# A decode block's backward pass: V transposed on TensorE as 32-bit words, and dP summed over even and odd features

## The chip, the cores and the metric

The kernel runs on one core of a Trainium2 chip. A core has five engines that run side by side and wait for each other through semaphores: TensorE (PE: matrix products and transposes, whose result always goes to the PSUM memory), VectorE (DVE), ScalarE (ACT), GpSimd (POOL) and SyncE (SP), which here only issues DMA transfers. A TensorE product has two halves in the profile: the load of the stationary operand (LDWEIGHTS, shown as PEld) and the pass of the moving operand (MATMUL, shown as PE). Sixteen DMA engines move data between the device memory (HBM) and the on-chip memory (SBUF, 128 partitions).

The metric is the time of one execution on the device in microseconds. The kernel before takes 1698.24 us (median of 3 runs, 1697.31 to 1698.51).

## The reference, cut to what matters

The program is one transformer block for a single new token, with its forward pass and the gradients of all inputs. There are 4 batches and 32 heads, so 128 pairs (b, h), called heads below and numbered s = 0 to 127; each has its own cached keys and values of 4096 rows by 128 features in bf16 (1 MB each).

```python
q      = (layernorm(x) @ wq)                      # per head: 128 features
scores = einsum("bhqd,bhkd->bhqk", q, k_cache) * Dh ** -0.5
p      = softmax(scores)
o      = einsum("bhqk,bhkd->bhqd", p, v_cache)
h      = x + o @ wo
h2     = h + (silu(hn @ w1) * (hn @ w3)) @ w2     # hn = layernorm(h)
```

The gradients with respect to the caches are as large as the caches. For one head, with dO the gradient of its output row:

```python
dP = V @ dO                        # 4096 numbers: each row of V times dO
dS = p * (dP - sum(p * dP)) * Dh ** -0.5
grad_V = outer(p,  dO)             # 4096 x 128, 1 MB
grad_K = outer(dS, q)              # 4096 x 128, 1 MB
```

The change is in how dP is computed. The forward pass and the outer products stay.

## The kernel before, in words

**Two passes over the caches.** The forward pass (up to about 675 us of the span) reads K and V of every head once. The small dense layers follow, and from about 695 us on the backward pass reads V of every head a second time and writes grad_V and grad_K: 3 MB of transfers for each head. All these transfers are issued from SP's queue, in the order of the program. SBUF holds an arena of 23 slots (`NSLOT`), each of which has room for one head's 1 MB; a load needs a free slot, and so does an outer product before it can be written. A slot becomes free again when a store has landed or when the V in it has been used.

**How a head of V lies in SBUF.** Partition p holds 32 consecutive cache rows (j = 0 to 31) with 128 features each: 4096 bf16 numbers.

**dP of the first 32 heads** (`SP = 32`). dP sums over features, and TensorE sums over partitions, so V has to be transposed. `V_T` (lines 791 to 801) does it in four groups of `GW = 8` rows: eight TensorE transposes of 128x128 bf16 blocks (line 800) fill one PSUM tile `pt_tps`, and ScalarE copies the tile back over the V it came from (line 801). There are two such PSUM tiles, so TensorE may be one group ahead of ScalarE. `front` (line 1212) runs the four groups for a head and then eight matmuls of 512 columns (line 1228) into the accumulator `dP_ps`. They are four wide in columns: each writes 32 of the 128 PSUM partitions (`tile_position=(0, 32 * c)`), and a small stationary operand `zd`, zero except for the column that belongs to this head, puts the head's dP into its own row. `dO_window` (line 1191) writes dO into `zd` on GpSimd, two heads ahead.

After four heads the accumulator is copied to SBUF (`rows_out`, line 1203), transposed by four 128x128 fp32 transposes (`rows_T`, line 1210), and `group_dS` (line 1239) makes dS from it on VectorE. `grad_V` and `grad_K` make the outer products on VectorE (line 806) and issue the stores (lines 817 and 1255). The copies `P_pairs` (line 1198) on GpSimd lay out p for grad_V.

**dP of the other 96 heads** goes by pairs of heads, 48 of them: one 2 MB load (line 1280) puts two heads side by side, 64 partitions each. `front_pair` (line 1292) has eight groups of eight transposes (line 1298) and copies (line 1299), then 16 matmuls (line 1313). `dO_pair` (line 1287) fills their stationary operand `zt` by one GpSimd copy (line 1290), `P2_pair` (line 1376) lays out p. `grad_pair` makes an outer product of 2 MB in one VectorE instruction (line 1379) and issues one store (line 1389).

**What sets the order.** The order on each engine is written out by hand by the loops at the end of the kernel (lines 1436 to 1493): for each head or pair the loads ahead, the front of a head five ahead (three pairs ahead), the grad_V outer products some heads ahead, the grad_K outer product, and now and then a step of side work (weight gradients). Each engine runs its instructions in that order.

Of the kernel before, what the change touches and what calls it, by code (L numbers as in the profile page):

```python
# [21 lines left out]
SP = 32  # L22
# [5 lines left out]
def kernel(  # L28
# [38 lines left out]
    GW = 8  # L67
# [724 lines left out]

    def V_T(s, ps, part=range(SJ // GW)):
        if s not in VTs:
            VTs[s] = V2s.pop(s)
        v = VTs[s].heads()
        for g in part:
            pt = ps.tile([P, GW, P], BF16, tag="tps", name="pt_tps")
            for i in range(GW):
                nc.tensor.transpose(pt[:, i, :], v[:, g * GW + i, :], ident_b[:])  # L800
            nc.scalar.copy(out=v[:, g * GW:(g + 1) * GW, :], in_=pt[:])  # L801
# [163 lines left out]
    with ExitStack() as c2:  # L965
# [221 lines left out]
        zd = [bw3.tile([P, 132], BF16, name=f"zd{i}", tag=f"zd{i}", bufs=1) for i in range(B)]  # L1187
        for i in range(B):
            nc.gpsimd.memset(zd[i][:], 0.0)

        def dO_window(s):
            if s < SP:
                nc.gpsimd.tensor_copy(out=zd[s % B][:, 32:132:67], in_=dOT_bf[:, s:s + 1].to_broadcast([P, 2]))
# [18 lines left out]
        def front(s):  # L1212
# [8 lines left out]
            VT = VTs[s].heads()  # L1221
# [3 lines left out]
            for u in range(2):  # L1225
                for c in range(4):
                    j0 = 8 * c + 4 * u
                    nc.tensor.matmul(rows["acc"][32 * c:32 * (c + 1), :], lhsT=zq_window(zd[hl], 2 * hl + u),
                                     rhs=VT[:, j0:j0 + 4, :], start=(hl == 0 and u == 0),
                                     stop=(hl == B - 1 and u == 1), tile_position=(0, 32 * c))  # L1230
# [8 lines left out]
        def group_dS(g):  # L1239
            i0 = g * B  # L1240
            T = rows.pop("T").rearrange("p jj (c m) -> p c m jj", c=4)
            t = rows.pop("t")[:, 0:B * SJ].rearrange("p (b j) -> p b j", b=B)
            t5 = t.rearrange("p b (c u jj) -> p b c u jj", c=4, u=2)
            for hl in range(B):
                nc.vector.tensor_scalar(out=t5[:, hl], in0=T[:, :, 2 * hl:2 * hl + 2, :], scalar1=c_rep[:, i0 + hl:i0 + hl + 1],
# [41 lines left out]
        def dO_pair(t):  # L1287
            if t < NT:
                s, s2 = two(t)
                nc.gpsimd.tensor_copy(out=zt[t % B][:, 32:34], in_=dOT_bf[:, s:s2 + 1:B])  # L1290

        def front_pair(t, mid):
            pl = t % 2
            v = pV[t].t[:, 0:2 * SJ * Dh].rearrange("p (j d) -> p j d", d=Dh)
            for g in range(2 * SJ // GW):
                pt = psT.tile([P, GW, P], BF16, tag="tps", name="pt_tps")
                for i in range(GW):
                    nc.tensor.transpose(pt[:, i, :], v[:, g * GW + i, :], ident_b[:])  # L1298
# [225 lines left out]
```

## Time and profile before

| | before |
|---|---|
| median of 3 runs | 1698.24 us |
| the profiled execution: span, first to last instruction | 1696.2 us |
| the profiled execution's own time: span and what lies around it (no time of its own is given; the median less the span is 2.0 us) | 1698.2 us |
| instructions | 37839 |
| PE busy | 1233.4 us (73%), 16228 matmuls, 16228 weight loads |
| DVE busy | 1234.4 us (73%) |
| ACT busy | 959.5 us (57%) |
| POOL busy | 336.9 us (20%) |
| moved | 707.45 MB, mean 417 GB/s |

A busy share is the time in which an engine had an instruction in work, divided by the span. An engine can be busy for 73% and still not set the time, because its work may lie beside something longer. So one looks next for the resource that has no idle time, then for the places where even that one has gaps, and asks what ended those gaps.

### The profile page before, as it was taken

Reading aid. Unit: us, or ns where it says so; the run is one execution under the profiler, and the core shown is the slowest. Engines: PE = TensorE matmul, PEld = TensorE weight load, DVE = VectorE, ACT = ScalarE, POOL = GpSimd, SP = SyncE. Lnnn points to the kernel's source line nnn. Section 1 sums busy time; section 2 is a strip of 40 time slices with the busy share of each in tenths; the row PEclk is TensorE's granted clock in tenths of the full one; section 3 lists DMA queues with packets and bytes.
Section 4 is the critical chain, followed back from the end, with each engine's and each line's share of the span. In section 5 each row is a group of like instructions: output and inputs, shape, how many; then the busy total and the mean of one; then the engine's idle time right before and its main releaser. Section 6 shows DMA issues by size and latency. Waiting matters only on the chain.

```text
span 1696.2 us, 37839 instructions
## 1 busy us (share of the span) xinstructions
PE 1233.4 (73%) x16228; PEld 943.4 (56%) x16228; DVE 1234.4 (73%) x1198; ACT 959.5 (57%) x1490; POOL 336.9 (20%) x583
## 2 busy tenths in 40 slices
PE   5889888888888888877876755667665666766650
PEld 4777667666677666655655544444444444444440
DVE  5989999999998997667766466575665655655683
ACT  3555544454454544677665555666665666666650
POOL 1211222222222222222231121011210102011120
PEclk8999999999999999899898689886678777676675
DMA  9999999999999999999999999999999999999995
GB/s 401 424 424 424 424 424 424 424 424 423 416 423 406 424 414 397 395 414 425 425 425 429 428 429 428 429 430 429 429 429 428 418 430 429 422 418 425 415 429 230
DMA packets 81000, 707.45 MB, mean 417 GB/s; under 512 B 8748, under 2 KB 12984, under 8 KB 15296
## 3 DMA queue, kind: packets, MB, share of 16 engines
q1 hardware_dynamic: 80416, 704.94, 99.0%
q8 instruction: 127, 2.08, 0.5%
q14 instruction: 41, 0.34, 0.0%
q0 software_dynamic: 416, 0.10, 0.0%
HBM read 422.59 MB, written 282.34 MB: 416 GB/s over the span
## 4 chain that ended last, share of the span: by engine, by line
DMA 46%; DVE 9%; PE 3%; issue 2%; ACT 1%; DVEq 0%; POOL 0%; SPq 0%; ACTq 0%
DMA out_dram<-arena 43%; DVE arena L1379 7%; DMA arena<-in_A_v_cache_dram 3%; DVE arena L806 1%; PE M_ps L472 1%; DVE arena L457 1%; PE pt_w L601 0%; ACT arena L1299 0%; ACT Pn L436 0%; DVEq L1519 0%; PE kP_ps L482 0%; DVE dPr L1326 0%; PE pt_tps L1298 0%; PE gu_ps L873 0%; PE dn_ps L904 0%
## 5 line engine op out<-in xcount | busy, mean ns | idle before, releaser
L1299 ACT COPY arena<-pt_tps 128x1024 bf16<-128x1024 bf16 x384 | 369.8, 1023 | 232.3 <-PE pt_tps L1298 231.6
L1298 PE MATMUL pt_tps<-ident_b,arena 128*128 128x128 bf16 x3072 | 308.1, 272 | 204.7 <-DMA arena<-in_A_v_cache_dram 149.4
L1298 PEld LDWEIGHTS <-arena 128*128 128x128 bf16 x3072 | 263.9, 125 | 304.2 <-DMA arena<-in_A_v_cache_dram 172.8
L1379 DVE TENSOR_TENSOR arena<-arena 128x8192 bf16<-128x8192 bf16 x48 | 212.5, 4427 | 205.1 <-DMA out_dram<-arena 202.3
L472 PE MATMUL M_ps<-arena 128*128 128x130 bf16 x4096 | 285.1, 222 | 42.9 <-DMA arena<-in_A_v_cache_dram 42.2
L457 DVE TENSOR_TENSOR arena<-arena 128x4096 bf16<-128x4096 bf16 x128 | 292.5, 2285 | 23.9 <-POOL arena L453 23.9
L472 PEld LDWEIGHTS <-arena 128*128 128x128 bf16 x4096 | 251.9, 99 | 64.0 <-DMA arena<-in_A_v_cache_dram 57.2
L1379 DVE TENSOR_TENSOR arena<-dS,arena 128x8192 bf16<-128x8192 bf16 x48 | 212.3, 4424 | 73.0 <-DMA out_dram<-arena 73.0
L364 DVE STREAM_TRANSPOSE arena<-arena 128x512 f32<-128x512 f32 (+1 forms) x321 | 250.7, 797 | 0.0
L359 ACT COPY arena<-pt_tps 128x1024 bf16<-128x1024 bf16 x128 | 129.5, 1012 | 188.9 <-PE pt_tps L358 150.5
L1376 POOL COPY arena<-arena 128x128 bf16<-128x128 bf16 x48 | 55.3, 1153 | 492.3 <-ACT arena L1353 286.3
L370 POOL TENSOR_TENSOR W<-qrep,wmask 128x128 bf16<-128x128 bf16 x128 | 120.2, 939 | 85.6 <-PE S_ps L390 70.8
L801 ACT COPY arena<-pt_tps 128x1024 bf16<-128x1024 bf16 x128 | 121.7, 1025 | 26.1 <-PE pt_tps L800 24.8
L453 POOL COPY arena<-P_all 128x64 bf16<-128x64 bf16 x128 | 32.7, 255 | 412.8 <-ACT P_all L447 409.8
L806 DVE TENSOR_TENSOR arena<-dS,arena 128x4096 bf16<-128x4096 bf16 x32 | 73.2, 2293 | 35.0 <-DMA out_dram<-arena 34.7
L800 PE MATMUL pt_tps<-ident_b,arena 128*128 128x128 bf16 x1024 | 78.5, 229 | 27.1 <-ACT arena L801 27.1
L1313 PE MATMUL dP_ps<-arena 128*32 128x512 bf16 x768 | 85.7, 484 | 7.6 <-ACT arena L1299 7.3
L800 PEld LDWEIGHTS <-arena 128*128 128x128 bf16 x1024 | 67.2, 104 | 37.5 <-issue 35.9
L447 ACT COPY P_all<-pt_P 32x64 bf16<-32x64 bf16 x256 | 52.1, 204 | 53.6 <-PE pt_P L443 51.4
L806 DVE TENSOR_TENSOR arena<-P,arena 128x4096 bf16<-128x4096 bf16 x29 | 66.4, 2295 | 19.8 <-DMA out_dram<-arena 19.8
L358 PE MATMUL pt_tps<-ident_b,arena 128*128 128x128 bf16 x1024 | 80.1, 222 | 0.0
L482 PE MATMUL kP_ps<-arena,onesw 128*32 128x512 bf16 x1024 | 79.6, 388 | 0.0
(245 smaller groups left out, 1576.5 us busy)
## 6 DMA issues: line engine op xcount, KB each, us to landing
out_dram<-arena SPq DMA_DIRECT2D x96, 2048.0 KB, 27.9
arena<-in_A_v_cache_dram SPq DMA_DIRECT2D x160, 1024.0 KB, 15.9
arena<-in_A_k_cache_dram SPq DMA_DIRECT2D x128, 1024.0 KB, 15.3
arena<-in_A_v_cache_dram SPq DMA_DIRECT2D x48, 2048.0 KB, 32.1
out_dram<-arena SPq DMA_DIRECT2D x72, 1024.0 KB, 20.2
arena<-in_A_wq_dram SPq DMA_DIRECT2D x8, 1024.0 KB, 14.4
arena<-in_B_w_dram SPq DMA_DIRECT2D x8, 896.0 KB, 15.3
out_dram<-arena SPq DMA_DIRECT2D x6, 896.0 KB, 28.4
```

Of the source, the lines that this page charges most:

```text
L359: nc.scalar.copy(out=KT[:, c * GW:(c + 1) * GW, :], in_=pt[:])
L364: nc.vector.transpose(out=KT[:, c * w_:(c + n) * w_], in_=Kn[:, c * w_:(c + n) * w_])
L370: nc.gpsimd.tensor_tensor(out=W[:, hl], in0=qrep[:, :, s:s + 1].to_broadcast([P, 4, 32]), in1=wmask[:, hl, None, :].to_broadcast([P, 4, 32 ...
L457: nc.vector.tensor_tensor(out=PK[:, :, 0:Dh].rearrange("p j (r t) -> p j r t", t=2), in0=Ks[s].heads().rearrange("p j (r t) -> p j r t", t=2),
L472: nc.tensor.matmul(hold["M"][:], lhsT=Vn[:, j, :], rhs=PK[:, j, :], start=(j == 0), stop=(j == SJ - 1))
L800: nc.tensor.transpose(pt[:, i, :], v[:, g * GW + i, :], ident_b[:])
L801: nc.scalar.copy(out=v[:, g * GW:(g + 1) * GW, :], in_=pt[:])
L806: nc.vector.tensor_tensor(out=dst.rearrange("p j (r t) -> p j r t", t=2), in0=col2[:, :, None, :].to_broadcast([P, SJ, Dh // 2, 2]), in1=r ...
L1298: nc.tensor.transpose(pt[:, i, :], v[:, g * GW + i, :], ident_b[:])
L1299: nc.scalar.copy(out=v[:, g * GW:(g + 1) * GW, :], in_=pt[:])
L1313: nc.tensor.matmul(rows["acc"][32 * c:32 * (c + 1), :], lhsT=zt[t % B][:, 32 - m:64 - m], rhs=v[:, j0:j0 + 4, :], start=(pl == 0 and u == ...
L1379: nc.vector.tensor_tensor(out=dst.rearrange("p (j r t) -> p j r t", r=Dh // 2, t=2), in0=col2[:, :, None, :].to_broadcast([P, 2 * SJ, Dh / ...
```

## The change

In PSUM and in the transposes a pair of neighbouring bf16 features is handled as one 32-bit word. A head then has 16 blocks of 128x128 words in place of 32 blocks of 128x128 bf16 numbers. A block covers two cache rows with 64 feature pairs each; after its transpose, partition i * 64 + r holds feature pair r of row i of the two. `words_T` does four such transposes for a group and the same ScalarE copy of 128x1024 bf16, whose destination now is four runs of 256 numbers. The groups are interleaved: group g takes blocks g, 4 + g, 8 + g and 12 + g.

Since even and odd features now lie side by side in one partition, dP is a sum of two matmuls: one reads the even features (every second bf16 number) with the even features of dO as stationary operand, the other the odd ones. The count of matmuls stays at 8 for a head and 16 for a pair. For this dO itself is needed in word order: `dO_words` makes it by four matmuls and a ScalarE copy, once ahead of the first head and once for the pairs. A stationary operand is now filled by two GpSimd copies of 64 partitions in place of one of 128. The transposed dP has its rows in another order, and `group_dS` and `group_dS_pair` read it accordingly.

```diff
+    def words_T(ps, v, g):
+        w = v.bitcast(FP32).rearrange("p (x r) -> p x r", r=Dh)
+        pt = ps.tile([P, GW, P], BF16, tag="tps", name="pt_tps")
+        ptw = pt.rearrange("p a b -> p (a b)").bitcast(FP32).rearrange("p (x q) -> p x q", q=P)
+        for jj in range(4):
+            nc.tensor.transpose(ptw[:, jj, :], w[:, 4 * jj + g, :], ident_f[:])
+        nc.scalar.copy(out=v.rearrange("p (x n) -> p x n", n=2 * Dh)[:, g:16:4], in_=pt.rearrange("p (x i) d -> p x (i d)", i=2))
+
+    def words_of(v, g, k):
+        return v.rearrange("p (x r t) -> p t x r", r=Dh, t=2)[:, k, g:16:4]
+
     def V_T(s, ps, part=range(SJ // GW)):
...
         for g in part:
-            pt = ps.tile([P, GW, P], BF16, tag="tps", name="pt_tps")
-            for i in range(GW):
-                nc.tensor.transpose(pt[:, i, :], v[:, g * GW + i, :], ident_b[:])
-            nc.scalar.copy(out=v[:, g * GW:(g + 1) * GW, :], in_=pt[:])
+            words_T(ps, VTs[s].t[:, 0:SJ * Dh], g)
...
+        def dO_words(dst, s0, s1):
+            ps = psrep.tile([P, 2, s1 - s0], FP32, tag="rep", name="dOw_ps")
+            for k in range(2):
+                for i in range(2):
+                    nc.tensor.matmul(ps[64 * i:64 * (i + 1), k, :], lhsT=ident_b[:, k:P:2], rhs=dOT_bf[:, s0:s1],
+                                     start=True, stop=True, tile_position=(0, 64 * i))
+            nc.scalar.copy(out=dst, in_=ps[:])
+
         def dO_window(s):
             if s < SP:
-                nc.gpsimd.tensor_copy(out=zd[s % B][:, 32:132:67], in_=dOT_bf[:, s:s + 1].to_broadcast([P, 2]))
+                for i in range(2):
+                    r_ = slice(64 * i, 64 * (i + 1))
+                    nc.gpsimd.tensor_copy(out=zd[s % B][r_, :, 2 * (s % B) + i], in_=dOw[r_, :, s])
...
-            for u in range(2):
+            for k in range(2):
                 for c in range(4):
-                    j0 = 8 * c + 4 * u
-                    nc.tensor.matmul(rows["acc"][32 * c:32 * (c + 1), :], lhsT=zq_window(zd[hl], 2 * hl + u),
-                                     rhs=VT[:, j0:j0 + 4, :], start=(hl == 0 and u == 0),
-                                     stop=(hl == B - 1 and u == 1), tile_position=(0, 32 * c))
+                    nc.tensor.matmul(rows["acc"][32 * c:32 * (c + 1), :], lhsT=zd[hl][:, k, :], rhs=words_of(v, c, k),
+                                     start=(hl == 0 and k == 0), stop=(hl == B - 1 and k == 1), tile_position=(0, 32 * c))
...
         def dO_pair(t):
             if t < NT:
                 s, s2 = two(t)
-                nc.gpsimd.tensor_copy(out=zt[t % B][:, 32:34], in_=dOT_bf[:, s:s2 + 1:B])
+                for i in range(2):
+                    r_ = slice(64 * i, 64 * (i + 1))
+                    nc.gpsimd.tensor_copy(out=zt[t % B][r_, :, ZP + 2 * i:ZP + 2 * i + 2], in_=zt[B][r_, :, s - SP:s2 - SP + 1:B])
...
             for g in range(2 * SJ // GW):
-                pt = psT.tile([P, GW, P], BF16, tag="tps", name="pt_tps")
-                for i in range(GW):
-                    nc.tensor.transpose(pt[:, i, :], v[:, g * GW + i, :], ident_b[:])
-                nc.scalar.copy(out=v[:, g * GW:(g + 1) * GW, :], in_=pt[:])
+                words_T(psT, v[g // 4], g % 4)
...
-            for u in range(4):
-                m = 8 * pl + 2 * u
-                for c in range(4):
-                    j0 = 16 * c + 4 * u
-                    nc.tensor.matmul(rows["acc"][32 * c:32 * (c + 1), :], lhsT=zt[t % B][:, 32 - m:64 - m], rhs=v[:, j0:j0 + 4, :],
-                                     start=(pl == 0 and u == 0), stop=(pl == 1 and u == 3), tile_position=(0, 32 * c))
+            for u in range(2):
+                m = 8 * pl + 4 * u
+                for k in range(2):
+                    for c in range(4):
+                        nc.tensor.matmul(rows["acc"][32 * c:32 * (c + 1), :], lhsT=zt[t % B][:, k, ZP - m:ZP - m + 32],
+                                         rhs=words_of(v[u], c, k), start=(pl == 0 and u == 0 and k == 0),
+                                         stop=(pl == 1 and u == 1 and k == 1), tile_position=(0, 32 * c))
...
+        dO_words(dOw[:], 0, SP)
         for s in range(2):
             dO_window(s)
...
                 if s + L == SP:
+                    dO_words(zt[B], SP, NH)
                     dO_pair(0)
```

Left out of the diff are the sizes of `zd`, `zt` and the new `dOw`, and the two dS functions, where only the order of the rows read changes.

## The prediction

> **What bounds the kernel now.** I read the slices of the page first, because they tell whether one resource has no gaps.
>
> ```profile
> PE   5889888888888888877876755667665666766650
> ACT  3555544454454544677665555666665666666650
> DMA  9999999999999999999999999999999999999995
> GB/s 401 424 424 424 424 424 424 424 424 423 416 423 406 424 414 397 395 414 425 425 425 429 428 429 428 429 430 429 429 429 428 418 430 429 422 418 425 415 429 230
> ...
> q8 instruction: 127, 2.08, 0.5%
> ```
>
> The DMA engines are full in 39 of 40 slices, TensorE and ScalarE in none. The change touches TensorE, ScalarE and GpSimd in the backward part, slices 17 to 40, so it can move the time only where the DMA engines have a gap there, or by what it adds to or takes from their work. Next come the gaps: the busy time by stretch.
>
> ```profile
> core 0: us, PE busy (x) PEld busy (x) DVE busy (x) ACT busy (x) POOL busy (x), PEclk, DMA share, GB/s
> 700.00:725.00 25.00, 17.25 (x189) 11.24 (x190) 20.46 (x15) 17.38 (x21) 11.32 (x22) 0.93 0.94 368
> 740.00:900.00 160.00, 126.16 (x1425) 92.31 (x1423) 110.52 (x85) 112.62 (x130) 43.17 (x49) 0.94 1.01 425
> 900.00:1600.00 700.00, 457.69 (x4361) 328.08 (x4359) 421.55 (x217) 439.03 (x542) 99.95 (x99) 0.74 1.01 426
> 1660.00:1670.00 10.00, 0.00 (x0) 0.00 (x0) 6.79 (x2) 0.00 (x0) 0.00 (x0) 0.50 1.01 429
> 1680.00:1690.00 10.00, 0.00 (x0) 0.00 (x0) 0.00 (x0) 0.00 (x0) 0.00 (x0) 0.50 0.06 26
> ```
>
> The DMA share (last column but one) is 1.01 from 740 to 1670 us; there TensorE and ScalarE may get slower or faster without moving the end, as long as they keep their pace: 3 MB a head at 425 GB/s is 7.4 us, 6 MB a pair at 426 is 14.8 us. Only the ramp of the backward part, 700 to 725 us, is below (0.94, 368 GB/s): what is lost there is not won back. From 1680 us on the share is 0.06, one engine of sixteen: all compute ended at 1667 us, and one DMA engine that is behind the others works off its queue to 1696. So the end of the compute isn't the end of the kernel: the other fifteen engines are done 13 us after it, the last one 29.
>
> **The change part by part.** The order on SP and VectorE stays, instruction for instruction; ScalarE gets 2 copies more, GpSimd 80, TensorE 2048 transposes less.
>
> *Transposes.* 4096 of 128x128 bf16 become 2048 of 128x128 fp32. The trace has fp32 transposes of that very shape, those of the dP rows. At the low granted clock (first two lines, at 1599 us) and at the full one:
>
> ```profile
> 1598.97 1.06 PE L1210 MATMUL dPT_ps<-ident_f,dPr 128*128 128x128 f32 x4
> 1599.82 1.06 PE L1298 MATMUL pt_tps<-ident_b,arena 128*128 128x128 bf16 x8
> ...
> 1625.71 0.66 PE L1210 MATMUL dPT_ps<-ident_f,dPr 128*128 128x128 f32 x4
> ...
> 1626.62 0.61 PE L1298 MATMUL pt_tps<-ident_b,arena 128*128 128x128 bf16 x8 [0.26 <-ACT arena L1299]
> ```
>
> Four fp32 transposes move what eight bf16 ones do and take 1.06 against 1.06 us, 0.66 against 0.61: equal per byte, with up to 0.05 us more until a group's last result. ScalarE takes 1.02 us for each group and TensorE 0.6 to 1.06, so a group's pace stays ScalarE's; per head one group's lead lies ahead of the first copy, +0.05 us. Bounds: 0.05 less (the rows are single groups, and may flatter the bf16 ones by as much) and 0.10 more, twice the difference seen.
>
> There is a rule that speaks against this part. The Trainium skill, "FP8 and Floating Point Precision", TensorE Precision Notes, gives true fp32 as four passes through the array. Read for transposes, four fp32 ones would cost as much as sixteen bf16 ones, about 2.1 us a group at the low clock, a pair's front would be 8 x 2.1 + 2.2 = 19 us against 14.8 of transfers, and 48 pairs would add some 200 us. The rows above show one MATMUL record for each fp32 transpose and no such price, so I go by the rows.
>
> *dP matmuls.* Same number, shape and stationary width; the moving operand now steps by two bf16 numbers. The forward score matmuls have both kinds beside each other, in line 390: those with `zq` read 32 numbers in a row, those with `W` every second one.
>
> ```profile
> 402.68 0.27 PE L390 MATMUL S_ps<-arena,zq 128*32 128x256 bf16 x1
> 402.68 0.29 PE L390 MATMUL S_ps<-arena,W 128*32 128x256 bf16 x3
> ...
> 403.44 0.27 PE L390 MATMUL S_ps<-arena,zq 128*32 128x256 bf16 x1
> 403.51 0.30 PE L390 MATMUL S_ps<-arena,W 128*32 128x256 bf16 x3
> ```
>
> Over eight steps `zq` goes from 402.68 to 403.44, 0.109 us a step, `W` to 403.51, 0.119: 9% more. A head's eight matmuls are two steps of four side by side, 512 columns each, some 0.43 us: +0.04 us; a pair twice that. Bounds 0 and +9%. All of it lies beside transfers, except in the ramp.
>
> *Evacuation copies.* 512 of the 1023 ns copies (128x1024 bf16 from PSUM) now write four runs of 256 numbers. The nearest row is the copy of the w1 and w3 transposes, 128x1024 in two runs of 512: 1031 ns. The far one, 128x896 with scattered numbers, is 1132 ns, 1.26 ns a number, which would make 1294. I take 1031 (the runs are long): +0.03 us a head. The far end would be +1.1 us a head, 6.3 instead of 5.2 us, still below the 7.4 of its transfers (fronts follow each other by 5.0 to 5.5 us in the timeline from 703 to 740 us); only the ramp would feel it, about seven heads, +7.6 us at most.
>
> *GpSimd.* The stationary fill is two copies, not one: a mean of 872 ns for a head and 995 for a pair, so 32 x 0.87 + 48 x 1.0 = +76 us on an engine that is 20% busy. The trace tells what these times are: the copy itself takes 0.19, the rest is waiting for VectorE.
>
> ```profile
> 714.29 6.73 DVE L806 TENSOR_TENSOR arena<-P,arena 128x4096 bf16<-128x4096 bf16 x3 [0.56 <-DMA out_dram<-arena]
> ...
> 716.64 2.24 POOL L1198 COPY P<-P_all 128x64 bf16<-128x64 bf16 x1 [2.48 <-DVE arena L806]
> 718.83 2.25 POOL L1193 COPY zd<-dOT_bf 128x2 bf16<-128x2 bf16 x1
> 721.01 0.23 POOL L1198 COPY P<-P_all 128x64 bf16<-128x64 bf16 x1
> ```
>
> While VectorE runs three outer products in a row, GpSimd gets one copy through for each. The Trainium skill, "SBUF — State Buffer", two separate sides, calls the port pair of the two engines an exclusive lock for a whole instruction, which agrees with the 2.24 and 2.25 us. So a second copy can hold up the `P` copy behind it, and with it grad_V on VectorE, by one more product, 2.3 us. `P` is laid out two heads ahead (over 4.6 us of VectorE's work) and VectorE itself waits for DMA between products, so I count 0 for it after the start and keep 2.3 us an occurrence for the rival. In the other direction VectorE's product at 703.22 us waited 1.59 us until GpSimd's first fills were through; two of the four fills are now doubled ahead of it and two beside it: +2 to +4 copies of 0.19, I take +0.4 us, with the first front waiting for the same fills.
>
> *dO in word order.* Four matmuls and a ScalarE copy ahead of the first head, at about 700 us, where TensorE waits 2.5 us for GpSimd and ScalarE is idle: nothing, as long as that cover holds; without it 0.5 us (0.3 of matmuls, 0.25 of copy). The second set at about 875 us lies beside full DMA engines: nothing.
>
> *Instruction fetch.* 16228 matmuls and as many weight loads are 32456 instructions; q8 moved 2.08 MB, 64 bytes for each: it is TensorE's instruction stream, on the same DMA engines. 2048 transposes fewer and 8 matmuls more leave 28376 instructions, 1.82 MB, 111 packets of 16 KB for 127. A packet's time is 0.5% x 16 x 1696 us / 127 = 1.07 us. 16 packets over 16 engines: -1.1 us for each. Bounds: nothing, if the engine that ends last fetches none of them, and -4.3 us, if it fetches four of them.
>
> *Sum.* Fetch -1.1; start +0.4; ramp, about seven heads x (0.05 + 0.04 + 0.03) = +0.8, of which half falls into the 6% gap or in waits for slots, +0.4. Together -0.3 us on the profiled execution's 1698.2 us (span 1696.2 and 2.0 around it), which is the median's 1698.24: **1697.9 us**. A measurement can tell about 0.2%, 3.4 us, from no change; this is inside.
>
> **The rivals.**
>
> 1. *No measurable change, transfers hide it* (the forecast). For it: DMA share 1.01 for 930 us.
> 2. *Faster through the DMA engines.* The last engine alone works from 1680 us. If it fetches four of the 16 dropped packets (-4.3 us) and the ramp costs nothing, 1698.2 - 4.3 = 1693.9. For it: the end is that one engine's; against it: nothing shows that it fetches more than its sixteenth.
> 3. *Slower through GpSimd in the ramp.* The doubled fills push `P` behind VectorE's next product; decisive once GpSimd is more than two products late. Two such waits, 2 x 2.3 us, plus the 0.8 of start and ramp, less the 1.1 of fetch: 1702.5. For it: one copy for each product in the rows above. Against: no wait for `P` appears in the list of waits before.
> 4. *TensorE becomes the bound.* If the fp32 transposes took twice their row in bursts, a group of four would take 2 x 1.06 = 2.1 us, a pair's front with its 16 dP matmuls (2.18 us in the timeline at 1573 us) 8 x 2.1 + 2.2 = 19 us against 14.8: 48 x 4.2 = 200 us, 1900. The rows at both clocks speak against it.
>
> **How the numbers follow.** Forecast 76%, rival 2 11%, rival 3 11%, rival 4 2%. The forecast's own terms run from 1695.0 (three packets fewer on the last engine, no cost) to 1700.4 (no gain from fetch, start 0.8, ramp 7 x 0.2 = 1.4). The range reaches rival 2 and rival 3: 1693.5 to 1702.5; outside lie rival 4 and parts of 2 and 3. Faster by over 0.2%: 0.12, rival 2 with a little of the first's edge; slower: 0.13, rivals 3 and 4; same: 0.75.
>
> **What the changed kernel's profile would show.** 14188 matmuls and weight loads for 16228, q8 near 111 packets and 1.82 MB; four fp32 transposes of 0.66 us (1.06 at the low clock) where eight were; evacuations near 1031 ns; fills doubled in number; DMA share still 1.01 from 740 to 1670 us; the ramp near 368 GB/s. It is wrong if the share falls below 1 between, if VectorE's waits for GpSimd grow in the ramp, if the evacuations near 1.3 us, or if the lone engine's tail after 1680 us changes its length by over 3 us.

## The result, and the profile after

The changed kernel takes **2079.48 us** (median of 4 runs, 2077.93 to 2083.09) against 1698.38 us for the kernel before (4 runs, 1697.31 to 1698.56): a ratio of **1.2249, 95% interval 1.2232 to 1.2267**. It is 381 us slower, where 1697.9 us and no measurable change were forecast, and far outside the range of 1693.5 to 1702.5.

The slices of the profiled execution (span 2079.1 us, 52 us a slice) show where. `PEclk` is the clock granted to TensorE and `DMA` the busy share of the 16 DMA engines, both in tenths (9 is 90% or more):

```profile
PEclk9999999999999555555555577655555555555555
DMA  9999999999999877667766977868889688867868
GB/s 404 424 424 424 424 424 424 424 417 423 415 406 405 345 243 246 250 251 256 292 263 263 388 312 327 348 250 341 325 340 374 242 315 337 336 272 283 333 278 358
...
q8 instruction: 112, 1.84, 0.3%
...
PE 26%; ACT 20%; issue 1%; DVE 0%; DMA 0%; DVEq 0%; ACTq 0%
```

The forward pass is as it was (404 to 424 GB/s). From the first slice of the backward part on, the DMA engines have gaps, 243 to 388 GB/s, and the granted TensorE clock sits at 0.5 for most of it. In the kernel before that row was

```profile
PEclk8999999999999999899898689886678777676675
```

The last line of the first view is the chain of work that ended last, in shares of the span: DMA, 46% in the kernel before, is gone from it, and TensorE (26%) and ScalarE (20%) have taken its place; the transposes and their copies are 19% each. By stretch (after the busy times: granted clock, DMA share, GB/s) the stretch from 740 to 900 us, which moved 425 GB/s before, and most of the pairs' stage:

```profile
740.00:900.00 160.00, 103.48 (x536) 71.28 (x535) 60.89 (x48) 68.47 (x73) 44.04 (x40) 0.50 0.73 253
...
1080.00:1600.00 520.00, 337.77 (x1865) 205.24 (x1865) 253.57 (x136) 262.82 (x299) 155.81 (x92) 0.59 0.79 322
```

The groups and the list of waits name the two partners (columns of a group: busy us, mean ns of one, idle before it; of a wait: us in total, times, longest):

```profile
L798 PE MATMUL pt_tps<-ident_f,arena 128*128 128x128 f32 x2048 | 542.7, 417 | 400.4 <-ACT arena L799 400.4
L799 ACT COPY arena<-pt_tps 128x1024 bf16<-128x1024 bf16 x512 | 517.5, 1012 | 577.9 <-PE pt_tps L798 573.8
```
```profile
ACT arena L799 <- PE pt_tps L798: 573.8, 494, 4.7
PE pt_tps L798 <- ACT arena L799: 400.4, 383, 2.4
```

The transposes wait for the copies and the copies wait for the transposes, in 383 and 494 of the 512 groups. In the kernel before, TensorE waited far less for them, 54.6 us for the copies of the pairs and 27.1 for those of the single heads:

```profile
PE pt_tps L1298 <- ACT arena L1299: 54.6, 137, 2.1
...
PE pt_tps L800 <- ACT arena L801: 27.1, 57, 0.7
```

The timeline of the changed kernel shows the turns group by group (start, duration, engine, and in brackets the idle time ahead and what ended it):

```profile
1324.81 1.11 PE L798 MATMUL pt_tps<-ident_f,arena 128*128 128x128 f32 x4 [1.10 <-ACT arena L799]
...
1325.96 1.01 ACT L799 COPY arena<-pt_tps 128x1024 bf16<-128x1024 bf16 x1 [1.20 <-PE pt_tps L798]
...
1327.03 1.12 PE L798 MATMUL pt_tps<-ident_f,arena 128*128 128x128 f32 x4 [1.10 <-ACT arena L799]
...
1328.18 1.01 ACT L799 COPY arena<-pt_tps 128x1024 bf16<-128x1024 bf16 x1 [1.21 <-PE pt_tps L798]
```

The two engines **take turns**. Four transposes, the copy, four transposes, the copy: 1327.03 - 1324.81 = 2.22 us for a group, the sum of 1.11 and 1.01 and 0.1 of hand-over, where the larger of the two was expected. The pairs' fronts follow each other by 20.3 us (the first dP matmul of a pair at 1096.8, the last at 2053.2 us, 47 intervals). Between these two times TensorE spent 391.8 us on transposes and 295.0 waiting for their copies, 14.6 us a pair; the 16 dP matmuls take 2.1, and side work with its waits makes up the rest. Before it was 15.7 us, the pace of the transfers. A head takes (1078.9 - 707.3) / 31 = 12.0 us where it took 6.4.

The program as built says why they take turns. In 384 of the 512 groups, all but the first of each head, the first transpose waits on a semaphore for ScalarE's copy of the group **just before** it; the trace counts 383 such waits. In the kernel before, the latest copy that a group waits for is the one two groups back, which emptied its PSUM tile. Nothing in the data asks for this: group g reads blocks g, 4 + g, 8 + g and 12 + g, the copy of group g - 1 writes blocks g - 1, 3 + g, 7 + g and 11 + g. The framework sets such waits where it takes a read and a write to overlap. The transposes read through a 32-bit view of the slot, the copy writes through a 16-bit view, and both step over the slot with gaps; which part of this it cannot tell apart was a matter for experiments, as was the low clock.

### The profile page after: what moved, and what is told of

Its sections match the earlier page's. It is cut to its first block, busy times and chain, and to the rows that moved or that the text cites. A ratio compares the mean times of both kernels' runs of the same rounds, so it can differ in the third digit from the quotient of the medians.

```text
span 2079.1 us, 33967 instructions
## 1 busy us (share of the span) xinstructions
PE 1464.9 (70%) x14188; PEld 1011.8 (49%) x14188; DVE 1229.4 (59%) x1198; ACT 989.9 (48%) x1492; POOL 519.0 (25%) x663
## 3 DMA queue, kind: packets, MB, share of 16 engines
q8 instruction: 112, 1.84, 0.3%
## 5 line engine op out<-in xcount | busy, mean ns | idle before, releaser
L798 PE MATMUL pt_tps<-ident_f,arena 128*128 128x128 f32 x2048 | 542.7, 417 | 400.4 <-ACT arena L799 400.4
L799 ACT COPY arena<-pt_tps 128x1024 bf16<-128x1024 bf16 x512 | 517.5, 1012 | 577.9 <-PE pt_tps L798 573.8
L798 PEld LDWEIGHTS pt_tps<-ident_f,arena 128*128 128x128 f32 x2048 | 355.3, 211 | 630.9 <-ACT arena L799 545.4
L472 PEld LDWEIGHTS <-arena 128*128 128x128 bf16 x4096 | 253.6, 99 | 58.2 <-DMA arena<-in_A_v_cache_dram 50.6
L1308 POOL COPY arena<-arena 64x4 bf16<-64x4 bf16 x96 | 166.4, 1733 | 277.7 <-PE dP_ps L1328 227.1
L359 ACT COPY arena<-pt_tps 128x1024 bf16<-128x1024 bf16 x128 | 129.4, 1012 | 186.6 <-PE pt_tps L358 149.0
L1342 DVE TENSOR_SCALAR dPr<-dPT_ps,c_rep 64x64 f32<-64x64 f32 x96 | 27.2, 284 | 307.4 <-PE dPT_ps L1228 306.3
L1397 POOL COPY arena<-arena 128x128 bf16<-128x128 bf16 x48 | 83.4, 1738 | 399.7 <-issue 348.6
L1211 POOL COPY zd<-dOw 64x2 bf16<-64x2 bf16 x64 | 62.5, 976 | 136.1 <-PE dP_ps L1245 133.8
L991 PE MATMUL gps<-arena 4*128 4x512 bf16 x110 | 59.9, 571 | 34.9 <-ACT arena L985 34.9
L358 PE MATMUL pt_tps<-ident_b,arena 128*128 128x128 bf16 x1024 | 80.5, 223 | 0.0
## 6 DMA issues: line engine op xcount, KB each, us to landing
out_dram<-arena SPq DMA_DIRECT2D x96, 2048.0 KB, 14.6
```

What stands on the lines that cost most here:

```text
L359: nc.scalar.copy(out=KT[:, c * GW:(c + 1) * GW, :], in_=pt[:])
L472: nc.tensor.matmul(hold["M"][:], lhsT=Vn[:, j, :], rhs=PK[:, j, :], start=(j == 0), stop=(j == SJ - 1))
L798: nc.tensor.transpose(ptw[:, jj, :], w[:, 4 * jj + g, :], ident_f[:])
L799: nc.scalar.copy(out=v.rearrange("p (x n) -> p x n", n=2 * Dh)[:, g:16:4], in_=pt.rearrange("p (x i) d -> p x (i d)", i=2))
L991: nc.tensor.matmul(ps[:, 0:n], lhsT=lhsT, rhs=rhs, start=True, stop=True)
L1308: nc.gpsimd.tensor_copy(out=zt[t % B][r_, :, ZP + 2 * i:ZP + 2 * i + 2], in_=zt[B][r_, :, s - SP:s2 - SP + 1:B])
```

## The experiments

**1 to 3. Which property of the groups brings the wait.** `contiguous_groups` is the changed kernel with consecutive blocks in a group (g and jj as in the new function):

```diff
-            nc.tensor.transpose(ptw[:, jj, :], w[:, 4 * jj + g, :], ident_f[:])
-        nc.scalar.copy(out=v.rearrange("p (x n) -> p x n", n=2 * Dh)[:, g:16:4], in_=pt.rearrange("p (x i) d -> p x (i d)", i=2))
+            nc.tensor.transpose(ptw[:, jj, :], w[:, 4 * g + jj, :], ident_f[:])
+        nc.scalar.copy(out=v.rearrange("p (x n) -> p x n", n=2 * Dh)[:, 4 * g:4 * g + 4], in_=pt.rearrange("p (x i) d -> p x (i d)", i=2))
```

> The changed kernel, but group g transposes and writes back the four neighbouring blocks 4g to 4g+3 instead of g, 4+g, 8+g, 12+g; the result in SBUF is the same. Theory (a lost overlap: each group's first transpose waits for ScalarE's copy of the group just before, so that TensorE and ScalarE take turns): the wait moves back by one group, the pace returns to ScalarE's 0.92 to 1.02 us a group, and the time to 1698 us, perhaps 1 us less for 16 fewer instruction packets; range 1694 to 1703. Rival A (32-bit transposes are slow by themselves): stays above 2000. Rival B (the doubled GpSimd fills hold up VectorE): stays above 1900, since all fills stay. Rival C (the matmuls that read every second number): stays above 1900.

`two_halves` interleaves within each half of the head only, so that consecutive groups lie in different halves:

```diff
-            nc.tensor.transpose(ptw[:, jj, :], w[:, 4 * jj + g, :], ident_f[:])
+            nc.tensor.transpose(ptw[:, jj, :], w[:, 8 * (g % 2) + g // 2 + 2 * jj, :], ident_f[:])
...
-        nc.scalar.copy(out=v.rearrange("p (x n) -> p x n", n=2 * Dh)[:, g:16:4], ...)
+        nc.scalar.copy(out=v.rearrange("p (x n) -> p x n", n=2 * Dh)[:, 8 * (g % 2) + g // 2:8 * (g % 2) + 8:2], ...)
```

> The changed kernel with groups interleaved only within a half of the head, the halves taking turns (blocks 0,2,4,6; 8,10,12,14; 1,3,5,7; 9,11,13,15). Two groups in a row never lie within each other's range; every evacuation still writes four scattered runs, and all transposes are 32 bits wide. Theory (lost overlap): 1697 us, 1694 to 1703, as with neighbouring blocks. Rivals A to C, and scattered writes: above 1900.

`bf16_interleaved` is the kernel before, bf16 transposes and all, with its groups interleaved by row pairs as in the changed kernel (shown for the single heads; the lines of the pairs change in the same way):

```diff
-                nc.tensor.transpose(pt[:, i, :], v[:, g * GW + i, :], ident_b[:])
-            nc.scalar.copy(out=v[:, g * GW:(g + 1) * GW, :], in_=pt[:])
+                nc.tensor.transpose(pt[:, i, :], v[:, 8 * (i // 2) + 2 * g + i % 2, :], ident_b[:])
+            nc.scalar.copy(out=v.rearrange("p (x i) d -> p x (i d)", i=2)[:, g:16:4], in_=pt.rearrange("p (x i) d -> p x (i d)", i=2))
```

> The kernel before, still with bf16 transposes, but with the groups interleaved as in the change (row pairs g, 4+g, 8+g, 12+g), and so with the same four runs of 256 numbers in each evacuation. Theory (the wait comes from interleaving together with the 32-bit view; in this program the transposes wait only for the copy two groups back): 1698 us, 1694 to 1702. Rival D (interleaving alone, its scattered writes or reads, is what costs): about 2050.

Measured, in this order: 1701.19 us, ratio 1.001 (0.9995 to 1.0025); 1696.58 us, 0.9994 (0.9976 to 1.0012); 1697.69 us, 0.9998 (0.9989 to 1.0007). All three are back at the time before. The single runs of the first two spread more than those of the kernel before (1696.1 to 1699.2 us beside them), from 1692.2 to 1704.0 and from 1688.2 to 1704.3; why is not known. Fp32 transposes, strided dP matmuls, doubled fills and the new layout of dS together cost nothing that can be measured in the time once the groups are apart, and interleaving alone costs nothing either. The loss needs word transposes and interleaving together. The waits of `contiguous_groups` in the backward part:

```profile
ACT arena L799 <- PE pt_tps L798: 247.4, 197, 9.3
...
PE pt_tps L798 <- ACT arena L799: 65.4, 177, 2.1
```

TensorE's 400.4 us have become 65.4, while the transposes themselves have the same median, 421 ns, in both kernels. In the timeline of `two_halves` TensorE runs the transposes of two groups in a row (eight, where the changed kernel had four) before it waits:

```profile
1306.56 1.94 PE L798 MATMUL pt_tps<-ident_f,arena 128*128 128x128 f32 x8 [6.11 <-DMA arena<-in_A_v_cache_dram]
...
1308.75 2.03 PE L798 MATMUL pt_tps<-ident_f,arena 128*128 128x128 f32 x8 [0.25 <-ACT arena L799]
```

**4. Are turns enough for such a loss?** `one_psum_buffer` is the kernel before with one PSUM tile for its groups, so that the same turns are forced on bf16 transposes:

```diff
-        psT = c2.enter_context(tc.tile_pool(name="psT2", bufs=2, space=bass.MemoryType.PSUM))
+        psT = c2.enter_context(tc.tile_pool(name="psT2", bufs=1, space=bass.MemoryType.PSUM))
```

> The kernel before with one PSUM buffer for the transposed groups of the backward part instead of two, and nothing else: bf16 transposes, and each group has to wait for the copy of the group before, as in the changed kernel. Theory (lost overlap is the whole of it): a group takes 1.01 (transposes at the low clock) + 1.01 (copy) + some 0.12 us of hand-over, 2.15 against 2.2 us in the changed kernel; 512 x 0.05 = 25 us less than 2079: 2055, range 2010 to 2090. Rival A (the 32-bit transposes cost): below 1850.

Measured: 2029.39 us, ratio 1.1958 (1.1941 to 1.1974), inside the expected range.

```profile
PEclk9999999999999755555555657665556555555555
DMA  9999999999999978777866879876889778877978
...
L1299 ACT COPY arena<-pt_tps 128x1024 bf16<-128x1024 bf16 x384 | 388.8, 1012 | 387.9 <-PE pt_tps L1298 387.8
L1298 PE MATMUL pt_tps<-ident_b,arena 128*128 128x128 bf16 x3072 | 364.9, 293 | 309.3 <-ACT arena L1299 309.2
```
```profile
740.00:900.00 160.00, 109.11 (x815) 79.70 (x815) 65.55 (x52) 69.09 (x74) 30.27 (x27) 0.51 0.76 269
```

It is the changed kernel's profile without the change: gaps in the DMA row, TensorE and ScalarE waiting for each other, and from 740 to 900 us a granted clock of 0.51, where the same instructions without turns had 0.94. The Trainium skill, "Perfetto Trace Analysis", Matmuls, asks that independent groups rotate through PSUM banks so that the evacuation of one overlaps the next one's matmuls. This pair of runs agrees and shows the price of not doing it, 331 us here; the changed kernel does rotate and still doesn't overlap.

**5. Is the low clock a cause or a consequence?** `filler_matmuls` gives TensorE eight more products for each group, into the new PSUM tile ahead of the transposes, which overwrite them:

```diff
+        for i in range(8):
+            nc.tensor.matmul(ptw[:, i % 4, :], lhsT=ident_b[:], rhs=ident_b[:], start=True, stop=True)
         for jj in range(4):
             nc.tensor.transpose(ptw[:, jj, :], w[:, 4 * jj + g, :], ident_f[:])
```

> The changed kernel with eight more bf16 products of 128x128 (identity by identity, written into the new PSUM tile and overwritten by the transposes) ahead of each group's four transposes, so that TensorE has work while it would wait for ScalarE's copy. The result is the same; 4096 matmuls more. Theory: the granted clock of 0.50 to 0.57 in the backward part is a consequence of the turn-taking, since TensorE pauses 1.1 us in each cycle of 2.2 us; with the pauses filled the clock rises, the four transposes take 0.66 us instead of 1.11, and a cycle is 0.66 + 1.01 + 0.09 = 1.76 us. Pairs then need 8 x 1.76 + 1.5 = 15.6 us against 14.8 of transfers (+38 us), heads about 12.1 - 4 x 0.44 - 0.5 = 9.8 against 6.4 (+110 us): 1850 us, range 1790 to 1900, with a clock over 0.8. Rival, the clock is low for another reason and doesn't rise with more work: the fillers fit into the pause (1.06 us at the low clock against 1.08), the cycle stays at 2.2 us or grows to 2.3, 2079 to 2130 us at a clock of 0.5 to 0.6.

Measured: 1873.76 us, ratio 1.1043 (1.1017 to 1.107). **With 4096 matmuls more the kernel is 206 us faster than the changed one.**

```profile
PEclk8999999999999998888978999999999999998997
```
```profile
740.00:900.00 160.00, 115.52 (x1190) 93.86 (x1190) 74.85 (x58) 81.02 (x88) 46.63 (x50) 0.89 0.87 306
```
```profile
1314.68 0.66 PE L800 MATMUL pt_tps<-ident_f,arena 128*128 128x128 f32 x4 [0.66 <-ACT arena L801]
1315.17 0.61 PE L798 MATMUL pt_tps<-ident_b 128*128 128x128 bf16 x8
1316.44 0.66 PE L800 MATMUL pt_tps<-ident_f,arena 128*128 128x128 f32 x4 [0.66 <-ACT arena L801]
```

The clock is up at 0.8 to 0.9, four transposes take 0.66 us in place of 1.11, and a turn is 1316.44 - 1314.68 = 1.76 us, as worked out beforehand. TensorE still pauses, but for 0.66 us in a turn in place of 1.10. So the low clock is a consequence of the turns: turns at a clock near the full one are worth 1873.8 - 1698 = 176 us, and the clock that they bring down another 206. This split is an estimate; what the added products themselves cost lies in the 176. It also leaves open whether the shorter pause lifts the clock or the kind of work, since the added products are no transposes. The time came out 24 us above the 1850 that had been expected, though inside the range. A pair takes (1842.5 - 1033.1) / 47 = 17.2 us, where 15.6 was put down, and a head (1019.1 - 704.0) / 31 = 10.2, where 9.8 was.

**6. Would a third PSUM tile help?** `three_psum_buffers` takes one from the pool of the side work, `psg`; `fewer_psg` shrinks `psg` alone:

```diff
-        psT = c2.enter_context(tc.tile_pool(name="psT2", bufs=2, space=bass.MemoryType.PSUM))
+        psT = c2.enter_context(tc.tile_pool(name="psT2", bufs=3, space=bass.MemoryType.PSUM))
...
-        psg = c2.enter_context(tc.tile_pool(name="psg", bufs=2, space=bass.MemoryType.PSUM))
+        psg = c2.enter_context(tc.tile_pool(name="psg", bufs=1, space=bass.MemoryType.PSUM))
```

> The changed kernel with three PSUM tiles for the groups in place of two (the space is taken from another pool, psg, which keeps one tile of two). Theory: what TensorE waits for is the copy of the group just before, whatever the number of tiles; so nothing changes, 2079 us, range 2060 to 2110, and TensorE's wait for ScalarE in front of the transposes stays at about 1.1 us for each group. Rival, the changed kernel is short of PSUM tiles: with a third one TensorE gets ahead again, 1700 to 1720 us.

> The changed kernel with one PSUM tile in place of two in the pool psg, which holds the side work's weight gradients, and two PSUM tiles for the groups as in the changed kernel. It tells what the 86 us are by which the kernel with three PSUM tiles for the groups is slower than the changed kernel (2165.4 against 2079.5). Theory: they are the side work's, whose products and copies (lines 991 and 985) take turns too with one tile; a third tile for the groups gave nothing: 2165 us, range 2145 to 2185. Rival, the third tile itself does harm, and psg is free: 2079 us, range 2070 to 2095.

Measured: 2165.44 us, ratio 1.2757 (1.2738 to 1.2776), and 2167.91 us, 1.2765 (1.2747 to 1.2782). The first lies outside its range, 2060 to 2110, so its own comparison doesn't stand by itself. The second gives the same time without a third tile: that tile is worth nothing, and the 86 us belong to the side work, which loses its second tile and takes turns as well. In `fewer_psg` the side work's 512-column products wait 86.5 us for their own copies, 34.9 in the changed kernel; these are some 52 of the 88 us by which `fewer_psg` is slower, and the rest isn't split up here:

```profile
L991 PE MATMUL gps<-arena 4*128 4x512 bf16 x102 | 58.1, 570 | 86.5 <-ACT arena L985 86.5
```

**7. How the loss splits.** `contiguous_pairs` gives consecutive groups to the pairs alone (`words_T(psT, v[g // 4], g % 4, True)`, with the two lines of experiment 1 behind that flag); the first 32 heads keep the interleaved ones.

> The changed kernel with consecutive blocks in a group (4g to 4g + 3) for the 48 pairs alone; the first 32 heads keep the interleaved groups. Theory: the wait is a matter of each group by itself, so the loss splits by stage. The head stage keeps its length of 387 us in the changed kernel (205 before, at a DMA share of 0.70), the pair stage is back at 426 GB/s and a share of 1.01: 1698 + 182 = 1880 us, range 1855 to 1905. Rival, the loss of the pair stage comes from a low clock or a lateness that the head stage leaves behind: the pair stage stays below a share of 0.9 at first, and the time is above 1920 us.

Measured: 1834.61 us, ratio 1.0811 (1.0793 to 1.0829), below the expected range. (The last three columns are again the clock, the DMA share and GB/s.)

```profile
695.00:1100.00 405.00, 265.27 (x1453) 182.36 (x1453) 169.77 (x121) 172.03 (x189) 98.29 (x116) 0.52 0.72 266
1100.00:1825.00 725.00, 462.14 (x2999) 297.98 (x2998) 451.70 (x230) 453.61 (x561) 120.48 (x142) 0.74 1.00 426
```

Each stage stands by itself, as the theory has it: 266 GB/s while the heads' groups are interleaved, 426 from the first pair on, with the clock up again. The heads cost 1834.6 - 1697.7 = 137 us, the pairs the other 245. The 182 us that had been expected for the heads were read wrongly: they compared the time from the first front to the last in the two kernels, but in the kernel before the stores of the last heads are still under way by then. Counted in transfers, 405 us at 266 GB/s are what takes 253 us at 425; 152 us are lost, of which some 15 come back, most of them at the end: the DMA share is low for the last 12 us (0.18), in the kernel before for the last 21 (0.20 and less), a sign that the one late DMA engine has had time to catch up.

**8. Do the doubled fills cost anything?** `doubled_fills` is the kernel before with each fill in two GpSimd copies of 64 partitions:

```diff
-                nc.gpsimd.tensor_copy(out=zd[s % B][:, 32:132:67], in_=dOT_bf[:, s:s + 1].to_broadcast([P, 2]))
+                for r_ in (slice(0, 64), slice(64, 128)):
+                    nc.gpsimd.tensor_copy(out=zd[s % B][r_, 32:132:67], in_=dOT_bf[r_, s:s + 1].to_broadcast([64, 2]))
...
-                nc.gpsimd.tensor_copy(out=zt[t % B][:, 32:34], in_=dOT_bf[:, s:s2 + 1:B])
+                for r_ in (slice(0, 64), slice(64, 128)):
+                    nc.gpsimd.tensor_copy(out=zt[t % B][r_, 32:34], in_=dOT_bf[r_, s:s2 + 1:B])
```

> The kernel before with each stationary operand filled by two GpSimd copies of 64 partitions in place of one of 128, 80 copies more, and nothing else. The changed kernel with consecutive groups moved 389 GB/s in its head stage (740 to 900 us) at a granted clock of 0.63, against 425 at 0.94 before, and gave it back later. Theory of the prediction: the doubled fills cost nothing, 1698 us, range 1695 to 1701, 425 GB/s in that stretch; then the lower rate there belongs to the fp32 transposes and their lower clock. Rival, the fills on GpSimd hold up the head stage: 390 to 410 GB/s in that stretch though the clock stays above 0.8, and 1700 to 1704 us.

Measured: 1698.17 us, ratio 1.0004 (0.9994 to 1.0013), with 425 GB/s from 740 to 900 us. The fills keep GpSimd busy for 132 us in place of 75, and the time stays. So the 389 GB/s of `contiguous_groups` in that stretch are not the fills'. The DMA engines are busy there (share 0.99), only each busy microsecond moves less. That stretch of `contiguous_groups`, and one at its end:

```profile
740.00:900.00 160.00, 130.89 (x871) 102.61 (x870) 94.30 (x73) 94.52 (x107) 65.98 (x56) 0.63 0.99 389
...
1680.00:1690.00 10.00, 0.00 (x0) 0.00 (x0) 0.00 (x0) 0.00 (x0) 0.00 (x0) 0.50 0.90 383
```

The second line shows why the time hardly tells: 160 us at 36 GB/s less are 5.8 MB, an estimated 14 us of transfers, and most of them find room at the end, where the kernel before had a share of only 0.06.

**9. Mixed views, or 32-bit blocks with gaps?** `word_copies` keeps the interleaved groups of the changed kernel and writes ScalarE's copy through the view that the transposes read, as 512 words in place of 1024 bf16 numbers; `contiguous_words` does the same with consecutive groups.

```diff
-        nc.scalar.copy(out=v.rearrange("p (x n) -> p x n", n=2 * Dh)[:, g:16:4], in_=pt.rearrange("p (x i) d -> p x (i d)", i=2))
+        nc.scalar.copy(out=w[:, g:16:4, :], in_=ptw[:])
```

> The changed kernel, its groups interleaved as they are, but ScalarE's copy written as 128x512 words of 32 bits, through the same view as the transposes read, in place of 128x1024 bf16 numbers. Theory: the wait for the copy just before comes from writing through a 16-bit view what is read through a 32-bit view, interleaved; with one view for both the writes of group g - 1 and the reads of group g are seen to be apart, TensorE is one group ahead again, and the DMA share is 1.01 from 740 us on: 1697 us, range 1690 to 1703. The copy should take about 0.59 us, as the copy of 128x512 fp32 out of dP_ps does, in place of 1.01; ScalarE's busy time falls by 512 x 0.42 = 215 us and the end doesn't move by that. Rival, interleaved 32-bit blocks are taken as overlapping whatever the view of the write: the turns remain, at 1.11 + 0.59 + 0.09 = 1.8 us for a group (1.34 at the full clock), 8 x 1.8 + 2.2 = 16.6 us for a pair and about 8.5 to 10.5 for a head, 1780 to 1880 us.

> Consecutive blocks in a group (4g to 4g + 3) and ScalarE's copy as 128x512 words. Against the kernel with consecutive groups and bf16 copies (1701.2 us, 389 GB/s at 740 to 900 us) it tells whether ScalarE's copy of 1.02 us set the pace of the head stage there. Theory: with copies of 0.59 us TensorE's 1.1 us a group at the low clock and the 7.4 us of transfers for a head are what is left; the head stage is back at 420 GB/s or more, 1696 us, range 1690 to 1700. Rival, TensorE at its lower clock (0.63) sets that stage's pace: 385 to 405 GB/s again, and 1699 to 1704 us.

Measured: **1692.39 us** (1691.74 to 1693.15), ratio 0.9967 (0.9954 to 0.9979), and 1692.01 us, 0.9965 (0.9951 to 0.9979). One line of the changed kernel, and it goes from 22% slower to a third of a per cent faster than the kernel before.

```profile
L798 PE MATMUL pt_tps<-ident_f,arena 128*128 128x128 f32 x2048 | 380.7, 349 | 266.4 <-DMA arena<-in_A_v_cache_dram 239.4 <-ACT arena L799 26.5
L799 ACT COPY arena<-pt_tps 128x512 f32<-128x512 f32 x512 | 289.2, 588 | 423.6 <-PE pt_tps L798 421.0 <-POOL zd L1211 1.3 <-DMA out_dram<-arena 0.8
```

TensorE now waits for V to arrive (239.4 us) and hardly for ScalarE (26.5): the transfers set the pace again. So it is not the gaps between the blocks that bring the wait, but the gaps together with two views of different width on the same slot. Which rule of the framework this is, the runs don't show.

The copy takes 588 ns in place of 1012 for the same bytes: (1012 - 588) / 512 = 0.83 ns an element, so that in these two kernels ScalarE's time goes by the elements. The Trainium skill, "ScalarE: Activation LUTs", What ACT_TABLE_LOAD costs, has the same 0.833 ns an element behind a fixed part.

`contiguous_words` differs from `contiguous_groups` in the copy alone, and its head stage is back at full rate, as its theory had it:

```profile
740.00:900.00 160.00, 122.46 (x986) 97.59 (x987) 112.34 (x85) 72.24 (x124) 41.83 (x64) 0.77 1.01 426
```

So the 389 GB/s of experiment 8 go with 16-bit copies beside word transposes. But the clock is 0.77 in place of 0.63, too, and ScalarE was busy for only 94.5 of the 160 us in `contiguous_groups`; that the copy set the pace there isn't shown.

**10. Whose are the 5.6 us?** `before_word_copies` is the kernel before with its copies as words and nothing else (the same edit in both places):

```diff
-            nc.scalar.copy(out=v[:, g * GW:(g + 1) * GW, :], in_=pt[:])
+            nc.scalar.copy(out=v[:, g * GW:(g + 1) * GW, :].rearrange('p j d -> p (j d)').bitcast(FP32), in_=pt.rearrange('p j d -> p (j d)').bitcast(FP32))
```

> The kernel before, its bf16 transposes unchanged, with ScalarE's 512 evacuation copies written as 128x512 words in place of 128x1024 bf16 numbers. It tells whose the 5.6 us are by which the changed kernel with word copies is faster than the kernel before (1692.4 against 1698.0). Theory: they come with the shorter copy (0.59 us in place of 1.02), since the two changed kernels without turns and with bf16 copies gave 1696.6 and 1701.2: 1693 us, range 1691 to 1695, with 428 GB/s or more from 900 to 1600 us. Rival, they belong to the transposes as words and the 15 instruction packets fewer, and the copies lie beside the transfers anyway: 1698 us, range 1696 to 1700, 426 GB/s.

Measured: 1703.5 us (1699.18 to 1704.7), ratio 1.0026 (1.0016 to 1.0037). Both expectations missed: the shorter copy by itself is no gain, and even a small loss. The transfers are without gaps in both kernels; two stretches of `before_word_copies`, and then the second of them in `word_copies`:

```profile
740.00:900.00 160.00, 121.09 (x1372) 93.54 (x1371) 110.43 (x84) 71.74 (x124) 32.92 (x47) 0.84 1.01 426
900.00:1600.00 700.00, 412.07 (x4307) 316.61 (x4307) 423.73 (x218) 295.03 (x536) 81.00 (x99) 0.76 1.01 425
```
```profile
900.00:1600.00 700.00, 432.24 (x2930) 298.70 (x2931) 425.32 (x218) 299.99 (x544) 140.04 (x149) 0.75 1.01 429
```

From 900 to 1600 us it is 425 against 429 GB/s at the same DMA share of 1.01 (426 in the kernel before). Over 700 us that is 6.5 us, most of the 11 between the two. What makes the same transfers 1% quicker or slower, when they are never short of work, the runs don't settle. In the medians the 5.6 us come only with word transposes and word copies together; single runs of `contiguous_groups` and `two_halves`, with 16-bit copies, reached 1692 and 1688 us as well. Why is open.

## Why the prediction was wrong

**The step that failed** is in the transposes' part: "so a group's pace stays ScalarE's". It took the larger of 1.02 us on ScalarE and 0.6 to 1.06 on TensorE, which holds as long as TensorE may be one group ahead. In the changed kernel the pace is the sum, 2.2 us, because a group's transposes wait for the copy just before. The two PSUM tiles are still there; what had gone was the independence of neighbouring groups. The prediction didn't name it as a condition, though the waits in the built program could be read before any run. Everything else follows from this one place: some 176 us for the turns, some 206 more for the clock that falls with them.

**The premise that the DMA engines hide it** ("may get slower or faster without moving the end, as long as they keep their pace") was right with its condition, and the condition broke: 20.3 us a pair against 14.8 of transfers. The first of its own signs of being wrong, a DMA share below 1 on the way, is what the profile shows (0.73 from 740 to 900 us). In the seven kernels in which the groups didn't wait for each other, not counting the kernel before itself, the median lies between 1692 and 1704 us whatever the transposes, copies and fills are.

**The fp32 transposes** were priced rightly. Four of them take 0.66 us at the full clock and 1.11 at the low one, against 0.66 and 1.06 from the rows. The 2.1 us that the prediction worked out from four passes, and set aside, did not come: `contiguous_groups` has all 2048 of these transposes with the same median, 421 ns, and is at 1701 us. Rival 4 ends nearest to the result (1900 us), but by a mechanism that these runs exclude; that it lies nearest is chance.

**The dP matmuls** were put at +9% for reading every second number. The shortest of them went from 376 to 385 ns and the typical one from 390 to 399 (`contiguous_groups`): +2.3%. Over-priced, and hidden either way.

**The evacuation copies**, put at 1031 ns, take 1012 in the changed kernel. Four runs cost no more than one: those of the pairs take 1023 ns in `bf16_interleaved` as in the kernel before.

**GpSimd.** The fills cost nothing (`doubled_fills`, +0.5 us with an interval across zero), as the forecast had it and rival 3 did not; this was measured on the kernel before.

**Instruction fetch.** 112 packets and 1.84 MB, 111 and 1.82 forecast. Its gain of 1.1 us is too small to be seen among the runs.

**The rivals.** None of the four named a wait between groups. Each of them looked for one engine or queue that is late; this loss came from two engines that are each busy for only half of a turn (TensorE 1.11, ScalarE 1.01 of 2.22 us).

## What to carry to other kernels

When an edit changes through which view a buffer is read or written, compare, ahead of any arithmetic on durations, which earlier instruction each stage waits for: here a wait that moved from two groups back to one turned a maximum into a sum, and the sum cost 22%. Reading and writing such a buffer through one view of one width, or giving neighbouring groups address ranges that don't interleave, brought the overlap back, each by itself. And where two engines of a pipeline each show long waits for the other while neither is full, look for turns first; a third buffer doesn't help against a wait that isn't for a buffer.

## What the hardware showed that was not expected

**Turns of 2.2 us bring the TensorE clock down to half.** `one_psum_buffer` has the instructions of the kernel before, and only the turns are new: from 740 to 900 us the granted clock is 0.51 in place of 0.94. In the changed kernel, where TensorE pauses for 1.1 us in a turn of 2.22, the backward part has 0.50 to 0.59, averaged by stretch, for over a millisecond. With products added into the pauses it has 0.86 to 0.97, and TensorE's real work gets faster by 1.11 / 0.66. About half of the loss of this change was this second effect. Where the limit lies is not shown, and the busy time alone doesn't set it: from 740 to 900 us `contiguous_groups`, without such turns, has a clock of 0.63 with TensorE busy for 130.9 us, `filler_matmuls` one of 0.89 with 115.5.

The Trainium skill, "TensorE: Matmul & The Clock Gate", Part 1, puts the fall of the clock behind an idle window of about 3.4 us. From 740 to 900 us the longest pause of TensorE in the changed kernel is 1.2 us, and the clock is low all the same, so pauses as long as that window are not needed here. The same page's section on depth-cycling through PSUM tells of short pauses that make the clock swing. That is nearer to these runs: in the pairs' stage the clock swings between 0.50 and 0.81 from one stretch of 20 us to another, though from 740 to 900 us it is 0.50 in every such stretch.

**A full DMA share doesn't fix the rate.** At a DMA share of 0.99 to 1.01, the stretch from 740 to 900 us moved 389 GB/s in `contiguous_groups`, 405 in `two_halves` and 425 or 426 in the kernel before and in those with word copies; the stretch from 900 to 1600 us moved 425 to 429. The loads of V and the stores are the same in all of them. What sets the rate is open.
